# Moving 512 tokens of a two-layer ELU product from plain blocks of 384 to a fourth block in seven products, with a recalibrated planner

## The chip, the cores and the metric

The kernel runs on one core of a Trainium2 chip. The metric is device microseconds for one launch: the median of three runs. A core has TensorE (PE, the matrix products), VectorE (DVE), ScalarE (ACT), GpSimd (POOL) and SyncE (SP, which only issues transfers here). Each engine works through its own list of instructions in order and waits for the others by semaphores.

## The reference

Random-feature attention on 8 x 8 heads of 576 tokens, then a two-layer network with ELU over the 4608 tokens.

```python
def phi(x):                                   # 64 -> 128 features
    proj = np.einsum('bhsd,md->bhsm', x, omega)
    h = proj - np.sum(x * x, axis=-1, keepdims=True) / 2.0
    return np.exp(h - np.max(h, axis=-1, keepdims=True)) / np.sqrt(m)
q_p, k_p = phi(q * scale), phi(k * scale)
kv = np.einsum('bhsm,bhsd->bhmd', k_p, v)
z = np.sum(k_p, axis=2)
attn = np.einsum('bhsm,bhmd->bhsd', q_p, kv) / (np.einsum('bhsm,bhm->bhs', q_p, z)[..., None] + 1e-06)

x = attn as [4608, 512]                       # 8 heads side by side
h = x @ w_in                                  # w_in  [512, 2048]
g = np.where(h > 0.0, h, np.exp(np.minimum(h, 0.0)) - 1.0)
out = g @ w_out                               # w_out [2048, 512]
```

The weights come as 64-bit floats and are converted on the chip. Every product of the network is made from three products of rounded parts: high x high, high x low, low x high.

## The kernel before

**Attention** goes by pairs of heads, 32 pairs (`pair`, i = 0 to 31). For a pair, k and q are projected on PE (`ppk`, `ppq`), a copy of the low part is taken out of PSUM (`p2k`, `p2q`, by ACT or DVE), DVE adds and takes the minimum (line 568), POOL corrects it, ACT makes the exponentials (474). PE makes `pkv`, DVE turns it, two transfers spread it (599, 607). DVE makes the denominators (740), POOL or DVE scales (`norm`), DVE turns the result into `qt` (820) and PE makes `pn` (842), which goes to DRAM as `xd`.

**The network** goes by blocks of tokens. `BLOCKS` names the plain ones: eight of 384 tokens, so that 1536 tokens are left for three blocks of 512 "in seven products". A plain block takes 16 steps (one for each 128 of the 2048 features). In a step, `layer1` makes 12 products `ph` of 384 columns (983 to 985), ACT and DVE make the ELU and its two parts (992 to 1004), and `layer2`, some 3.4 steps later, makes three products of 512 columns into `acc` for each 128 tokens (1017 to 1019), so 9 for a block of 384. The first three blocks go in two halves, SPLIT, while the weights are converted. In the text the plain steps are numbered through: 128 of them before (8 x 16), steps 0 to 47 in the first three blocks.

**A block in seven products** (`units`, `fetch`, `wide1`, `wide2`) makes each product of 2 x 2 sub-blocks with seven products in place of eight. It has 8 steps; a step holds 84 products of 256 columns (1369, 1527, 1339) for 256 features. It needs sums of the weights, made once: `prepare` reads converted `w_in` back into `rw`, makes sums of it and writes `w1t` (16 writes, two for each j = 0 to 7, 1084), through three buffers "raw"; `prepare2` makes sums `tw` of `w_out` in SBUF. `fetch` brings `wp` from `w1s` and `w1t` for each step. `units` makes sums of the tokens (`xw`, `xy`).

**The order** comes from `Plan`. Every piece of work is entered with an engine, a cost in ns, a due time and often a second or third engine with a penalty (`ALT`). `Plan.order` runs through time: at each moment a free engine takes, of what is ready by the planner's own costs, the piece that is due first. What comes out is a fixed list for each engine; the chip then follows these lists. So the costs (`mm`, `act`, `dve`, `pool`, `DMA_LAT`, `DMA_RATE`) and the due times (`PD0` and `PDS` for the pairs, `PREP0` and `PREP`, `TWO0` and `TWO`, `SEG`, `STEP` ...) set nothing but the order and the engine of each piece. In the kernel before, a product of 384 columns was entered at 162.5 ns and one of 512 at 215.8 ns.

Of the kernel before, what the change touches and what calls it, by code (L numbers as in the profile page):

```python
# [62 lines left out]
SUM = 0.873  # L63
UNIT0, UNIT1 = 0.25, 3.77
FETCH = 14.688
BT = [-0.751, -0.373, 0.719, 0.06, 0.525, 0.7, 0.865, -0.155, -0.328, 1.177, -1.344, 0.575, -1.141, 0.489]
AT = (0.0, 0.337, 0.844, 0.312, 0.229, 0.181, 0.386)

LAG = 3.4


PAIR0 = 6.45
DUE_LOAD, DUE_K, DUE_KV, DUE_Q = 9.63, 24.93, 17.79, 16.94
# [1 line left out]
TAIL = 14.17
TAIL2 = -0.54


CONV1 = 13.95
CONV_STEP = 0.16  # L80
CONV2 = 1.14
CONV3 = 41.4
# [1634 lines left out]
```

## Time and profile before

| | us |
|---|---|
| median of 3 runs | 1006.68 (1005.38 to 1009.03) |
| profiled execution | 1008.6 |
| its span, first to last instruction | 1006.8 |
| PE busy in the span | 979.3 |
| DVE busy | 843.7 |
| ACT busy | 766.2 |
| POOL busy | 557.8 |

Matmuls overlap in the profile, so that PE's busy time says that it had work, not that it ran at its pace. The pace is read from the starts of matmuls that follow each other. On DVE and ACT, too, the duration of one instruction is some 0.08 us longer than the distance to the next start when they follow closely. A stretch of the program is looked at by its own row: length, busy time of each engine, clock.

### The profile page before, as it was taken

The page shows a single profiled execution, that of the slowest core. Times are in us where ns is not written, and L with a number is a line of the kernel's source. Part 1 is how long each engine was busy: PE and PEld are TensorE (multiplying, and loading weights), DVE is VectorE, ACT ScalarE, POOL GpSimd, SP SyncE. Part 2 cuts the span into 40 slices and gives each one's busy share as a digit, 9 for nine tenths or more (in the row PEclk, how much of TensorE's full clock was granted, in tenths as well). Part 3 has the DMA queues.
Part 4 walks back from the last instruction along what each step waited for, and adds up shares of the span by engine and source line. Part 5 has one row for each costly group of instructions (what it writes and reads, how often), then busy time and mean ns, then how long its engine had stood idle before and what let it go on. Part 6 is the DMA issues. An engine that isn't in the chain of part 4 may idle for free.

```text
span 1006.8 us, 24315 instructions
## 1 busy us (share of the span) xinstructions
PE 979.3 (97%) x7806; PEld 881.6 (88%) x7806; DVE 843.7 (84%) x3077; ACT 766.2 (76%) x2064; POOL 557.8 (55%) x745
## 2 busy tenths in 40 slices
PE   6999999999999999999999999999999999999997
PEld 5887889888888888888888888887888999999997
DVE  5999978786778967887889888889999889779766
ACT  5999876877568888788887878786555688877774
POOL 0667676776457676677667766685442232223221
PEclk8999999999999999999999999999999999999999
DMA  6656777857766777676776767666888885775762
GB/s 178 181 183 214 238 247 254 270 200 245 232 216 218 232 224 225 202 230 195 252 226 189 242 206 234 203 208 232 268 311 290 289 298 176 238 240 191 239 196 76
DMA packets 93264, 226.27 MB, mean 225 GB/s; under 512 B 23056, under 2 KB 35024, under 8 KB 93136
## 3 DMA queue, kind: packets, MB, share of 16 engines
q1 hardware_dynamic: 93136, 224.70, 69.0%
q8 instruction: 63, 1.03, 0.4%
q14 instruction: 65, 0.53, 0.2%
HBM read 187.43 MB, written 37.22 MB: 223 GB/s over the span
## 4 chain that ended last, share of the span: by engine, by line
PE 69%; DVE 16%; DMA 8%; ACT 3%; issue 2%; SPq 1%; POOL 1%; DVEq 0%; POOLq 0%; ACTq 0%
PE acs L1527 8%; PE ph L983 7%; PE ph L985 6%; PE ph L984 6%; PE acc L1017 6%; PE acc L1018 6%; PE acc L1019 6%; PE A L1369 5%; PE B L1369 4%; PE pn L842 3%; PE pkv L622 2%; PE ppq L554 2%; PE ppk L554 2%; DVE rw L394 2%; DMA rw<-w1s 1%
## 5 line engine op out<-in xcount | busy, mean ns | idle before, releaser
L983 PE MATMUL ph<-xh,w1c 128*128 128x384 f32 x512 | 176.8, 345 | 4.6 <-DVE g L1004 3.0
L984 PE MATMUL ph<-xl,w1c 128*128 128x384 f32 x512 | 172.3, 336 | 1.0 <-DVE xl L807 1.0
L985 PE MATMUL ph<-xh,w1c 128*128 128x384 f32 x512 | 172.3, 336 | 0.0
L1017 PE MATMUL acc<-w2h,g 128*128 128x512 f32 x384 | 154.3, 402 | 0.2
L1018 PE MATMUL acc<-w2l,g 128*128 128x512 f32 x384 | 151.6, 395 | 0.0
L1019 PE MATMUL acc<-w2h,g 128*128 128x512 f32 x384 | 151.5, 394 | 0.0
L983 PEld LDWEIGHTS ph<-xh,w1c 128*128 128x128 f32 x512 | 96.2, 188 | 17.0 <-DVE g L1004 7.3
L984 PEld LDWEIGHTS ph<-xl,w1c 128*128 128x128 f32 x512 | 96.3, 188 | 3.8 <-DVE xl L807 1.4
L992 ACT ACTIVATE e<-ph 128x384 f32<-128x384 f32 x128 | 62.6, 489 | 44.4 <-PE ph L985 43.4
L394 POOL TENSOR_TENSOR hq<-hq,den 128x512 f32<-128x512 f32 (+1 forms) x96 | 81.1, 854 | 27.3 <-DVE den L749 23.5
L985 PEld LDWEIGHTS ph<-xh,w1c 128*128 128x128 f32 x512 | 96.2, 188 | 0.0
L996 DVE SCALAR_TENSOR_TENSOR ph<-e,ph 128x384 f32<-128x384 f32 x128 | 71.2, 556 | 25.5 <-ACT e L993 24.3
L394 POOL TENSOR_TENSOR gq<-yh,gq 128x256 fp32r<-128x256 f32 x49 | 42.7, 871 | 85.1 <-ACT gq L389 67.0
L1019 PEld LDWEIGHTS acc<-w2h,g 128*128 128x128 f32 x384 | 72.1, 188 | 16.9
L1017 PEld LDWEIGHTS acc<-w2h,g 128*128 128x128 f32 x384 | 72.0, 188 | 16.3 <-issue 6.3
L740 DVE CUSTOM_DVE_ANT_0 junk<-hq,pz 128x128 f32<-128x128 f32 (+1 forms) x320 | 74.5, 279 | 11.6 <-PE pz L718 9.3
L394 POOL TENSOR_TENSOR tk<-xk,tk 64x576 fp32r<-64x576 f32 x45 | 64.1, 1424 | 31.5 <-ACT tk L389 12.6
L474 ACT ACTIVATE hk<-hk,nbk 128x128 f32<-128x128 f32 x216 | 68.4, 390 | 17.0 <-POOL nbk L580 16.7
L1018 PEld LDWEIGHTS acc<-w2l,g 128*128 128x128 f32 x384 | 72.1, 188 | 8.6
L474 ACT ACTIVATE hq<-hq,nbq 128x128 f32<-128x128 f32 x216 | 68.5, 391 | 14.4 <-POOL nbq L580 13.6
L394 POOL TENSOR_TENSOR tq<-xq,tq 64x576 fp32r<-64x576 f32 x46 | 65.8, 1431 | 23.6 <-ACT tq L389 11.5
L1004 DVE TENSOR_TENSOR g<-ph,g 128x384 fp32r<-128x384 f32 x128 | 70.4, 550 | 5.7 <-PE pn L842 1.8
(222 smaller groups left out, 2814.7 us busy)
## 6 DMA issues: line engine op xcount, KB each, us to landing
w1c<-w1s SPq DMA_DIRECT2D x112, 512.0 KB, 4.5
wp<-w1t SPq DMA_DIRECT2D x48, 512.0 KB, 4.0
raw_w<-in_w_dram SPq DMA_DIRECT2D x32, 512.0 KB, 4.3
xk<-in_kx_dram SPq DMA_DIRECT2D x24, 576.0 KB, 4.2
xq<-in_qx_dram SPq DMA_DIRECT2D x24, 576.0 KB, 4.7
wp<-w1s SPq DMA_DIRECT2D x24, 512.0 KB, 4.5
v<-in_v_dram SPq DMA_DIRECT2D x32, 325.0 KB, 3.3
w1s<-w1c SPq DMA_DIRECT2D x16, 512.0 KB, 4.2
```

Of the source, the lines that this page charges most:

```text
L394: (nc.vector if e == "DVE" else nc.gpsimd).tensor_tensor(*args)
L474: nc.scalar.activation(h()[:, j, :], src(j), AF.Exp, bias=nb()[:, j:j + 1], scale=-1.0)
L740: nc.vector.tensor_tensor_reduce(out=junk()[r], in0=h()[r, j, :], in1=pz()[r, a * P:(a + 1) * P], scale=1.0, scalar=EPS, op0=ALU.mult, op1 ...
L983: nc.tensor.matmul(ph(), wh, xh[:, c, o:o + n], start=(c == 0), stop=False)
L984: nc.tensor.matmul(ph(), wh, xl[:, c, o:o + n], start=False, stop=False)
L985: nc.tensor.matmul(ph(), wl, xh[:, c, o:o + n], start=False, stop=(c == NC - 1))
L996: lambda: nc.vector.scalar_tensor_tensor(ph(), e()[:, 0:n], -1.0, ph(), ALU.add, ALU.max), (p, e), (p,),
L1017: nc.tensor.matmul(a(), g[0]()[:, ts], w2h[:, f], start=(f == f0), stop=False)
L1018: nc.tensor.matmul(a(), g[0]()[:, ts], w2l[:, f], start=False, stop=False)
L1019: nc.tensor.matmul(a(), g[1]()[:, ts], w2h[:, f], start=False, stop=(f == f1 - 1))
L1369: nc.tensor.matmul(o, at(a, i), u[b][:, i], start=(start and fresh_bank and i == 0 and n == 0), stop=(i == 1 and n == 2), skip_group_check ...
L1527: nc.tensor.matmul(bank()[:, z * TH:(z + 1) * TH], g()[:, a * TH + z * P:a * TH + z * P + P], w(b), start=(j == 0 and z == 0 and m == 0), ...
```

## The change

Plain blocks become six of 384 tokens and one of 256; the tokens left for blocks in seven products become 2048, so four blocks of 512. A plain step of the last block now has 12 products of 256 columns and 6 of 512. There are 112 plain steps. All due times and most penalties are replaced; a product's cost becomes 0.467 n - 6.2 ns (173.1 for 384, 232.9 for 512), POOL's costs rise, a transfer's end is entered later (`DMA_POST`).

```diff
-BLOCKS = [TB] * 8
+BLOCKS = [TB] * 6 + [256]
...
-MLP0 = 37.61
+MLP0 = 26.35
...
-STEP_SA, STEP_S = 9.344, 8.511
-LAG2 = 1.848
-PD0, PDS = 122.22, 19.83
+STEP_SA, STEP_S = 8.851, 9.878
+LAG2 = 17.388
+PD0, PDS = 122.202, 15.999
...
-SLOT = {3: 0, 4: 1, 5: 2, 6: 1, 7: 0}
+SLOT = {3: 0, 4: 1, 5: 2, 6: 0}
...
-PREP0, PREP = -101.339, 8.8
-TWO0, TWO = -37.142, 7.995
+PREP0, PREP = -100.636, 9.727
+TWO0, TWO = -21.196, 7.375
...
+DMA_POST = 2461.004
...
-LOAD2, K2, KV2, Q2 = 61.21, 47.49, 31.23, 34.51
+LOAD2, K2, KV2, Q2 = 55.648, 47.228, 27.084, 26.03
...
-    DMA_LAT, DMA_RATE = 1100.0, 360.0
+    DMA_LAT, DMA_RATE = 500.0, 320.0
...
-                    end[best] = dma + self.DMA_LAT
+                    end[best] = dma + DMA_POST
...
 def mm(n, m=1):
 
-    return m * (n / 2.4 + 2.5)
+    return m * (0.467 * n - 6.2)
...
 def pool(n):
-    return 40 + 2.33 * n
+    return 120 + 2.22 * n
...
-                op("PE", 872 if g < 2 else 240, d, mms, [*((x, a, 2) for a in range(2)), of], (p,))
+                op("PE", 930 if g < 2 else 290, d, mms, [*((x, a, 2) for a in range(2)), of], (p,))
...
-        op("POOL", 3 * pool(2 * M) + 2 * pool(M), due + 0.5, sums, parts, (zs, (zu, 1)))
+        op("POOL", 3480, due + 0.5, sums, parts, (zs, (zu, 1)))
```

The rest of the diff is of this kind: costs of single pieces and the table `ALT`. The lines of the changed kernel stand two lower than before (998 for 996).

In the middle of the plain blocks, DVE's list at the projection of pair 20's q (`hq_20`), before. The copy `p2q_20` out of PSUM isn't in it: ACT has it.

```order
L568 ISA hq_20_6768,nbq_20_6769<-ppq_20_0_6743,p2q_20_0_6762 128x128
L568 ISA nbq_20_6769 128x1
L568 ISA hq_20_6768,nbq_20_6769<-ppq_20_0_6743,p2q_20_0_6762 128x128
L568 ISA nbq_20_6769 128x1
L996 SCALAR_TENSOR_TENSOR ph_71_6714<-e_71_6748,ph_71_6714 128x384
L749 RECIPROCAL den_19_6751<-den_19_6751 128x4
```

The same place after. Plain step 64 stands where step 71 stood, so the pairs come earlier in the plain blocks.

```order
L570 ISA hq_20_6622,nbq_20_6623<-ppq_20_2_6608,p2q_20_2_6627 128x128
L570 ISA nbq_20_6623 128x1
L998 SCALAR_TENSOR_TENSOR ph_64_6524<-e_64_6592,ph_64_6524 128x384
L393 COPY p2q_20_3_6654<-ppq_20_3_6645 128x256
L393 CAST g_64_0_6665<-ph_64_6524 128x384
L570 ISA hq_20_6622,nbq_20_6623<-ppq_20_3_6645,p2q_20_3_6654 128x128
```

A copy `p2q` of this pair has moved from ACT to DVE; of the 96 copies of 256 columns DVE now has 48, against 20 before.

At the end of the plain blocks, DVE's list in steps 122 and 123, before: the ELU of a step (`ph`, two `g`) with the first block's token sums.

```order
L996 SCALAR_TENSOR_TENSOR ph_122_11302<-e_122_11325,ph_122_11302 128x384
L394 TENSOR_TENSOR xw_0_0_11061<-xw_0_1_11148,xw_0_0_11061 128x2x256
L391 CAST g_122_0_11356<-ph_122_11302 128x384
L1004 TENSOR_TENSOR g_122_1_11365<-ph_122_11302,g_122_0_11356 128x384
L394 TENSOR_TENSOR xy_0_11370<-xw_0_1_11148,xw_0_0_11061 128x512
L394 TENSOR_TENSOR xl_148<-xw_0_0_11061,xl_148 128x512
L394 TENSOR_TENSOR xw_0_1_11148<-xw_0_1_11148,xy_0_11370 128x2x256
L394 TENSOR_TENSOR xl_148<-xy_0_11370,xl_148 128x512
L996 SCALAR_TENSOR_TENSOR ph_123_11345<-e_123_11377,ph_123_11345 128x384
```

The same stretch after, in steps 106 to 108 of 256 tokens:

```order
L998 SCALAR_TENSOR_TENSOR ph_106_10728<-e_106_10755,ph_106_10728 128x256
L393 CAST g_106_0_10771<-ph_106_10728 128x256
L396 TENSOR_TENSOR w2_qh_1_156<-tw_4_10725,w2_qh_1_156 128x256
L1006 TENSOR_TENSOR g_106_1_10780<-ph_106_10728,g_106_0_10771 128x256
L396 TENSOR_TENSOR xy_0_10791<-xw_0_1_10574,xw_0_0_10564 128x512
L396 TENSOR_TENSOR w2_qh_1_156<-tw_4_10725,w2_qh_1_156 128x256
L393 CAST xl_148<-xy_0_10791 128x512
L396 TENSOR_TENSOR xw_0_1_10574<-xw_0_1_10574,xy_0_10791 128x2x256
L998 SCALAR_TENSOR_TENSOR ph_107_10775<-e_107_10803,ph_107_10775 128x256
L393 CAST g_107_0_10823<-ph_107_10775 128x256
L1006 TENSOR_TENSOR g_107_1_10833<-ph_107_10775,g_107_0_10823 128x256
L396 TENSOR_TENSOR rw_3_1_10733<-rw_3_1_10733 128x512
```

The pieces of a step are narrower, and weight sums (`tw` for `w2_qh`, `rw`) now stand among the last steps together with the token sums.

In the first block in seven products, SP's list from the last pair of writes of the weight sums (`rw_7`, for step 7) on, before (`wp_0_5_1` is the second transfer for step 5 of block 0):

```order
L1084 DMA w1t_143<-rw_7_0_11792 128x1024
L1084 DMA w1t_143<-rw_7_1_12032 128x1024
L1296 DMA wp_0_5_0_12221<-w1s_142 128x1024
L1296 DMA wp_0_5_1_12260<-w1t_143 128x1024
L1296 DMA wp_0_5_2_12301<-w1t_143 128x1024
L1301 DMA wq_0_7_12348<-w1s_142 128x2x256
L1239 DMA xw_1_0_12358<-xd_144 128x2x512
L1296 DMA wp_0_6_0_12363<-w1s_142 128x1024
L1239 DMA xw_1_1_12373<-xd_144 128x2x512
L1296 DMA wp_0_6_1_12409<-w1t_143 128x1024
```

The same writes after:

```order
L1298 DMA wp_0_6_0_11761<-w1s_142 128x1024
L1298 DMA wp_0_6_1_11794<-w1t_143 128x1024
L1086 DMA w1t_143<-rw_7_0_11469 128x1024
L1086 DMA w1t_143<-rw_7_1_11680 128x1024
L1298 DMA wp_0_6_2_11881<-w1t_143 128x1024
L1303 DMA wq_1_0_11891<-w1s_142 128x2x256
L1241 DMA xw_1_1_11934<-xd_144 128x2x512
L1298 DMA wp_0_7_0_11938<-w1s_142 128x1024
L1298 DMA wp_0_7_1_11963<-w1t_143 128x1024
L1298 DMA wp_0_7_2_12033<-w1t_143 128x1024
```

The writes for step 7 stood ahead of the transfers for step 5; now they stand between those for step 6.

## Rows read from the trace of the kernel before

**Rows 1.** The page, part 1: busy us of each engine.

```profile
PE 979.3 (97%) x7806; PEld 881.6 (88%) x7806; DVE 843.7 (84%) x3077; ACT 766.2 (76%) x2064; POOL 557.8 (55%) x745
```

**Rows 2.** Busy time by stretch: length, PE, PEld, DVE, ACT, POOL, clock, DMA.

```profile
0.00:63.50 63.50, 52.74 (x399) 45.20 (x399) 49.15 (x170) 49.49 (x141) 26.85 (x30) 0.95 0.61 175
63.50:279.60 216.10, 211.03 (x1334) 183.10 (x1333) 181.25 (x588) 166.31 (x406) 144.75 (x156) 1.00 0.72 236
279.60:639.40 359.80, 359.33 (x3166) 315.41 (x3164) 296.23 (x1431) 296.34 (x825) 248.52 (x380) 1.00 0.69 219
639.40:803.90 164.50, 158.94 (x1185) 141.35 (x1185) 151.89 (x472) 103.68 (x278) 81.58 (x113) 1.00 0.78 266
803.90:1006.80 202.90, 197.24 (x1730) 196.53 (x1728) 165.17 (x418) 150.38 (x418) 56.09 (x69) 1.00 0.65 206
842.20:917.90 75.70, 75.39 (x663) 75.18 (x663) 63.95 (x163) 59.12 (x163) 20.71 (x25) 1.00 0.70 224
```

**Rows 3.** The same view, one of the stretches of 20 us.

```profile
720.00:740.00 20.00, 19.65 (x157) 17.41 (x157) 19.41 (x41) 12.29 (x32) 5.89 (x7) 1.00 0.76 283
```

**Rows 4.** Timeline of PE in a plain step: start us, duration us, instruction.

```profile
743.71 0.34 PE L985 MATMUL ph<-xh,w1c 128*128 128x384 f32 x1
743.88 0.39 PE L1017 MATMUL acc<-w2h,g 128*128 128x512 f32 x1
744.11 0.39 PE L1018 MATMUL acc<-w2l,g 128*128 128x512 f32 x1
```

**Rows 5.** Timeline of PE in a block in seven products.

```profile
868.93 0.84 PE L1369 MATMUL A<-xh,wq 128*128 128x256 f32 x6
869.61 0.84 PE L1369 MATMUL B<-xl,wp 128*128 128x256 f32 x6
```

**Rows 6.** The chain that ended last, a pair's larger products: start us, us, what.

```profile
392.99 1.30 PE pn L842 x64
400.41 1.24 PE pkv L622 x20
```

**Rows 7.** Timeline of DVE in the middle of the plain blocks.

```profile
405.37 0.55 DVE L1004 TENSOR_TENSOR g<-ph,g 128x384 fp32r<-128x384 f32 x1
405.84 0.28 DVE L568 CUSTOM_DVE_ANT_0 hk<-ppk,p2k 128x128 f32<-128x128 f32 x1
...
407.85 0.42 DVE L391 COPY p2k<-ppk 128x256 f32<-128x256 f32 x1
408.19 0.70 DVE L820 STREAM_TRANSPOSE qt<-hq 128x512 f32<-128x512 f32 x1
```

**Rows 8.** Groups by line and shape, the copies p2q: count, busy us, mean ns, idle before.

```profile
L389 ACT COPY p2q<-ppq 128x256 f32<-128x256 f32 x76 | 27.7, 367 | 8.7 <-PE ppq L554 8.1
L391 DVE COPY p2q<-ppq 128x256 f32<-128x256 f32 x20 | 8.4, 421 | 5.4 <-PE ppq L554 5.3
```

**Rows 9.** Timeline of DVE, the last transposes of a pair.

```profile
431.24 0.50 DVE L820 STREAM_TRANSPOSE qt<-hq 128x128 f32<-128x128 f32 x2
```

**Rows 10.** Timeline of PE, the product that takes them.

```profile
432.74 1.37 PE L842 MATMUL pn<-qt,zk 32*64 32x160 f32 x64
```

**Rows 11.** Whom PE waited for: us in total, times, longest us.

```profile
PE ph L983 <- DVE g L1004: 3.0, 7, 0.7
...
PE ph L983 <- DMA w1c<-w1s: 0.5, 1, 0.5
```

**Rows 12.** Timeline of SP, three of the writes of weight sums.

```profile
755.83 0.92 SPq L1084 DMA_DIRECT2D w1t<-rw  x2
...
772.43 0.73 SPq L1084 DMA_DIRECT2D w1t<-rw  x1
...
789.67 1.31 SPq L1084 DMA_DIRECT2D w1t<-rw  x1
```

**Rows 13.** Timeline of DVE in the first block in seven products.

```profile
783.73 0.97 DVE L394 TENSOR_TENSOR rw<-rw 128x256 f32<-128x256 f32 x1
...
785.50 0.41 DVE L394 TENSOR_TENSOR rw<-rw 128x256 f32<-128x256 f32 x1
```

More of the change, by code (lines that the diff above doesn't have):

```diff
@@ L47 @@
 NNAT = dict(k=8, q=8)
-MLP0 = 37.61
-SEG = [6.25, 7.76, 3.48, 4.4, 2.75, 6.34]
-STEP = 5.52
-STEP_ATT = 5.44
-STEP_SA, STEP_S = 9.344, 8.511
-LAG2 = 1.848
-PD0, PDS = 122.22, 19.83
+MLP0 = 26.35
+SEG = [6.324, 7.876, 3.468, 4.4, 2.814, 6.61]
+STEP = 5.526
+STEP_ATT = 5.491
+STEP_SA, STEP_S = 8.851, 9.878
+LAG2 = 17.388
+PD0, PDS = 122.202, 15.999
 NSA = 1
-SLOT = {3: 0, 4: 1, 5: 2, 6: 1, 7: 0}
+SLOT = {3: 0, 4: 1, 5: 2, 6: 0}
 NP3 = 29
-PREP0, PREP = -101.339, 8.8
-TWO0, TWO = -37.142, 7.995
[L63 to L73, printed above, removed]
-LOAD2, K2, KV2, Q2 = 61.21, 47.49, 31.23, 34.51
[L75 to L82, printed above, removed]
+PREP0, PREP = -100.636, 9.727
+TWO0, TWO = -21.196, 7.375
+SUM = 1.791
+UNIT0, UNIT1 = 15.907, 4.301
+FETCH = 14.91
+BT = [-0.005, 0.805, 1.476, -0.381, 0.298, -0.265, 1.847, -0.58, -2.137, -0.081, -0.546, -1.317, -1.924, -0.352]
+AT = (0.0, -1.177, 0.709, 0.638, 0.39, 0.064, 0.462)
+LAG = 3.37
+DMA_POST = 2461.004
+PAIR0 = 5.932
+DUE_LOAD, DUE_K, DUE_KV, DUE_Q = 12.998, 24.825, 16.694, 15.838
+LOAD2, K2, KV2, Q2 = 55.648, 47.228, 27.084, 26.03
+TAIL = 11.864
+TAIL2 = -12.969
+CONV1 = 13.966
+CONV_STEP = 0.379
+CONV2 = -1.69
+CONV3 = 44.38
 SPLIT = (0, 8, 16)
 NHALF = 3
-DUE_Z = 15.42
+DUE_Z = 16.328
 NEARLY = 6
@@ L539, in project @@
             op(
-                "POOL", pool(S), due - 4 + a,
+                "POOL", 1495, due - 4 + a,
                 lambda e, r=r, o=o, cs=cs: tt(e, y()[o, cs], x()[r, 0], y()[r, cs].bitcast(F32), ALU.subtract),
@@ L557, in view @@
                 return p().rearrange("p (a x) -> p a x", a=2)
-            op("PE", mm(256, n), d, mms, [(y, a, z) for a in range(2) for z in "hl"] + ["oh", "om"], (p,))
+            op("PE", 118 * n + 10, d, mms, [(y, a, z) for a in range(2) for z in "hl"] + ["oh", "om"], (p,))
             op(
@@ L580, in bias @@
                     nc.gpsimd.tensor_tensor(m, m, q, ALU.subtract)
-                op("POOL", 2 * pool(4), d + 1.3, bias, [sq, *((nb, g, e) for e in range(5))], ((nb, g),))
+                op("POOL", 550, d + 1.3, bias, [sq, *((nb, g, e) for e in range(5))], ((nb, g),))
                 exps(g, js, lambda j: h()[:, j, :], d + 1.5, [(h, g, e) for e in range(5)])
@@ L626, in kv_swapped @@
         parts = parts_of(i, "k")
-        op("PE", 5 * 216, due, mms, [*parts, v], (p,))
+        op("PE", 1340, due, mms, [*parts, v], (p,))
         op("DVE", dve(M), due + 1.2, lambda: nc.vector.transpose(kvf, p()[:, 0:M]), (p,), (("kvf", i % 2),))
@@ L683, in kv @@
         parts = parts_of(i, "k")
-        op("PE", 220, due, last, [*parts, v], ((p, 0), (p, 1)))
+        op("PE", 240, due, last, [*parts, v], ((p, 0), (p, 1)))
         for a in range(2):
@@ L776, in finish @@
             d = due - 5 + g
-            op("PE", 109 * n, d, turn, ((h, "n", g),), (p,))
+            op("PE", 115 * n + 20, d, turn, ((h, "n", g),), (p,))
             op(
@@ L796, in finish @@
         d = due - 2
-        op("PE", 4 * mm(S) + 200, d, mms, [*((qh, g) for g in range(3)), ("kvf", i % 2)], [p for _, _, p in halves])
+        op("PE", 1250, d, mms, [*((qh, g) for g in range(3)), ("kvf", i % 2)], [p for _, _, p in halves])
         for half, (qs, n, p) in enumerate(halves):
@@ L846, in output @@
         op(
-            "PE", 4 * mm(4 * N) + 200, due, mms, [*((qt, g) for g in range(3)), *((zk, "kv", e) for e in range(4))], banks
+            "PE", 1400, due, mms, [*((qt, g) for g in range(3)), *((zk, "kv", e) for e in range(4))], banks
         )
```

4 lines of the change are left out of this document (2 added, 2 removed).

## The prediction

> **What bounds the kernel now.** The page's busy times come first: PE 97%, DVE 84%, ACT 76% [rows 1]. A busy PE need not run at its pace, so I then read the starts of matmuls. In a plain step a product of 384 columns is followed after 0.17 us and one of 512 after 0.23 us [rows 4]; the medians of all such distances are 0.174 and 0.233. In the blocks in seven products six products of 256 columns take 0.68 us, 0.113 each [rows 5]. A pair's `pn` and `pkv` take 1.30 and 1.24 us [rows 6], its 18 projections and `pz` about 0.12 each: 4.9 us.
>
> Then the span by stretches [rows 2], cut where PE begins plain steps 0, 40 and 104 and step 4 of the first block in seven products. I call them A to E (the last row of the group is one whole block in seven products and belongs to E). Counting PE's instructions at their pace gives the work in each, and the rest is lost:
>
> A 44.4 of 63.5, lost 19.1. B 203.3 of 216.1, lost 12.8. C 353.2 of 359.8, lost 6.6. D 154.4 of 164.5, lost 10.1. E 195.9 of 202.9, lost 7.0. Together 951.2 of work and 55.6 lost.
>
> So PE is the bound from the first plain step on. Where DVE has room, PE loses under 2%: in C DVE is busy 296 of 360, 82%. In D it is busy 151.9 of 164.5, 92%, and PE loses 6.5% [rows 2]. That pair of rows carries the prediction.
>
> **The work that goes and comes on PE.** A plain step of 384 tokens is 12 x 0.174 + 9 x 0.233 = 4.185 us; two blocks are 32 steps, 133.9 us, which go. The block of 256 brings 16 steps of 12 x 0.113 + 6 x 0.233 = 2.754 us, 44.1. The fourth block in seven products brings 75.7, read off a whole one [rows 2]. Net 44.1 + 75.7 - 133.9 = -14.1 us. The matmuls are f32 at one pace in both kernels, the clock stands at 1.00 (2.4 GHz) from the first plain step on [rows 2], and no stretch of the change would lower it. This gain is sure as work; the question is how much more PE waits.
>
> **DVE in the middle.** The order puts the pairs closer: before, one pair for 3.65 plain steps; after, one for 2.9 (20 pairs in steps 40 to 95, where it was 18 in steps 40 to 103). PE work of the new C (steps 40 to 95), counted over the list: 56 x 4.185 + 20 x 4.9, some 333 us. DVE: a step's three passes of 384 at 0.47 us [rows 7] are 1.41, 56 of them 79 us. What is left of the old C's 296 after 64 x 1.41 = 90 is 206, over 18 pairs 11.4 each; 20 pairs are 229. To these come the pieces that the new list hands to DVE: 28 copies `p2q` of 0.34 us [rows 7, 8], and ten subtractions of 576 columns that POOL had, about 1.0 each, so 20 us over 24 pairs, 16 here. Sum 79 + 229 + 16 = 324 us, 97% of PE's 333 (it was 82%). ACT, counted likewise, comes to 90%.
>
> What PE would lose at that load: below, the old C's 1.9% (6.6 us); above, the old D's 6.5% (21.7 us). Reasons for the lower end: the chain from a pair's last `ppq` to its `pn` was long before because due times made it so, and `pn` came 1 to 2 us after the last transpose was done (431.24 + 0.50 to 432.74) [rows 9, 10]; counted over the new list, 20.5 us of PE work lie between the two (28.8 before) with 16.1 us of DVE work (21.4 before), 79% against 74%: tighter, but not by much. I take 9 us lost, 2 to 3 above the old C.
>
> **DVE at the change of stage.** The new D runs from plain step 96 to the end of the first block in seven products. PE work there: 16 x 2.754 + 75.7 + the rest of the last pairs and of the block before, counted 125.4. DVE, counted over the list: 16 for the steps, 7 for the last pairs, 51 for the weight sums `rw` and `tw`, 16 for token sums, 45 for the seven products; 135, and 139.9 by the ratio that the old D has (147 counted, 151.9 busy). Here DVE has more to do than PE, because the weight sums are as many as before while the plain steps that hid them are 8 fewer and narrower. DVE can be busy 97% while PE is busy 98% [rows 3], so 139.9 takes 144 at the least; PE may be ahead by about a plain step, 3 us. I take 141.5, lost 16, where the old D lost 10.1. Ends: 136 (lost 11, some of the sums run over into the second block, whose stretch has room: DVE 64 of 75.7 [rows 2]) and 151.5 (lost 26, DVE at the old D's 92%).
>
> **The rest.** A and B hold the same attention work: DVE 57 and 171 us counted against 58 and 167, PE 44.4 and 201.7 against 44.4 and 203.3; at most 2 us either way, priced +0.5. One more block in E adds what the middle ones lose, under 0.5. The later ends of transfers in the planner move only SP's order; PE waited for weights 0.5 us in all [rows 11], so this part is worth nothing by itself. POOL stays under 85%.
>
> By the span: 1006.8 - 14.1 + 2.5 + 6 + 0.5 + 0.5 = 1002.2. The profiled execution lay 1.8 above its span and 1.9 above the median of the runs, so 1002 in those terms, and I round the ends' drift into **1001.5 us**.
>
> **Weight sums on SP.** After, the writes for step 7 stand between the transfers for step 6; before, ahead of those for step 5. The sums came every 17 us (755.83, 772.43, 789.67) [rows 12], while a step takes 9.5. SP waits in order, so a late `rw` holds `wp` behind it, and PE with it. The new order leaves about 1.5 steps less between a write and its reader, some 14 us. I price it at nothing, hidden by the half step that is left and by the transfers already fetched; if this cover is gone it costs up to 9 us: the last three sums at 17 us are 51, and the new list gives them 4.5 steps, 42.
>
> **Rivals.** *The lists tell true* (18%): the new list's PE costs, 173 and 233 ns, are those of the trace, so pieces are placed where they are really ready, C loses no more than before, and DVE's excess in D runs over into the second block. 1006.8 - 14.1 + 1 + 1 = about 994.5. Against it: 97% on DVE.
>
> *It cancels* (20%): C loses 14 and D 18, 1006.8 - 14.1 + 7.5 + 8 = 1008: no change that can be measured.
>
> *DVE takes over, slower* (17%): DVE keeps only the 92.3% of the old D. C takes 324 / 0.923 = 351, lost 18, D 151.5, lost 26: 1006.8 - 14.1 + 11.5 + 16 = 1020. It decides from the point where DVE's busy share of C stays under 95% although PE has gaps. For it: all three engines are above 90% there, with two `ph` banks between them.
>
> *The SP queue* (6%): 9 us in the first block in seven products on top of the forecast, 1010.
>
> *DVE blocked by POOL* (7%): of two DVE pieces `rw` of one shape one took 0.97 us, the other 0.41 [rows 13]. If 20 more of the weight sums meet such a neighbour in the new D, where DVE is the bound, at 0.55 each that is 11 us, 1012. The Trainium skill, page "SBUF — State Buffer", section "SBUF: two separate sides", names what could do it: a DVE instruction with two inputs in SBUF and a GpSimd instruction that reads SBUF contend for one pair of ports, and the later one waits for the whole of the other. The trace agrees as far as the pair of durations above goes.
>
> *It does not do what it says*: excluded for the blocks (the list holds 112 plain and 32 steps of seven products); true for the late transfers, which is priced at nothing.
>
> **How the numbers follow.** My forecast, 996 to 1003.7, has 32%, the better rival 18%, together 50% for faster by over 0.3%; within 0.3% (about what a measurement of this kernel can tell from no change) 20%; slower 30% from the last three rivals. Range 989 to 1020: below lies the case where A and B gain too, above the one where DVE and SP both fail. The likeliest case's own range is 994 to 1008.
>
> **What would show it.** Right: plain steps 40 to 95 take 339 to 346 us with DVE at 93% or more; from step 96 to the second block in seven products 136 to 146; a middle block 75.7; the stretch to plain step 40 within 3 us of 279.6. Wrong: PE waiting for DVE pieces (`g`, `qt`) by more than 20 us in C, or for `wp` in the first block in seven products; or DVE's pieces much longer than before at the same shapes.

## The result and the profile after

The changed kernel takes 1020.62 us (median of 4 runs, 1020.26 to 1023.59), the kernel before 1006.24 beside it: a ratio of 1.0144, 95% interval 1.0117 to 1.0172. It is slower by 1.4%, clear of the noise, where 1001.5 was forecast, and lies 0.6 us above the range. The profiled execution took 1023.59 with a span of 1021.8, 15.0 more than before.

Page of the changed kernel, part 1 (busy us of each engine, to be laid beside [rows 1]):

```profile
PE 980.9 (96%) x8094; PEld 882.1 (86%) x8094; DVE 907.6 (89%) x3255; ACT 787.6 (77%) x2144; POOL 561.3 (55%) x747
```

PE is busy as long as before, but does less: counted at its pace its list holds 937.8 us, 13.4 fewer than 951.2. DVE is busy for 64 us more.

Busy time by stretch in the changed kernel, A to E as the prediction cuts them and then D in four parts (columns as in [rows 2]):

```profile
0.00:63.20 63.20, 52.72 (x399) 45.23 (x399) 48.77 (x170) 51.20 (x143) 25.60 (x29) 0.95 0.63 183
63.20:278.60 215.40, 209.41 (x1331) 181.72 (x1330) 187.34 (x600) 173.28 (x421) 145.51 (x160) 1.00 0.71 235
278.60:627.10 348.50, 345.50 (x3235) 297.48 (x3235) 324.60 (x1586) 297.28 (x851) 266.65 (x416) 1.00 0.69 224
627.10:780.60 153.50, 138.13 (x1085) 123.69 (x1083) 144.20 (x381) 97.09 (x268) 59.60 (x70) 0.99 0.81 281
780.60:1021.80 241.20, 235.11 (x2052) 233.96 (x2052) 202.72 (x523) 168.78 (x462) 63.93 (x73) 0.99 0.63 203
627.10:665.30 38.20, 33.18 (x299) 26.38 (x298) 36.75 (x132) 23.08 (x68) 20.05 (x28) 1.00 0.83 297
665.30:688.80 23.50, 20.97 (x125) 18.38 (x124) 21.77 (x45) 9.39 (x24) 10.36 (x12) 0.93 0.72 248
688.80:737.00 48.20, 42.02 (x323) 38.91 (x322) 44.91 (x108) 31.32 (x85) 14.86 (x17) 1.00 0.90 307
737.00:780.60 43.60, 41.96 (x345) 40.02 (x343) 40.77 (x100) 33.30 (x93) 14.33 (x13) 1.00 0.75 255
```

Work counted over PE's list, and what is lost against it:

| | work | took | lost | lost before |
|---|---|---|---|---|
| A | 44.4 | 63.2 | 18.8 | 19.1 |
| B | 201.7 | 215.4 | 13.7 | 12.8 |
| C | 333.9 | 348.5 | 14.6 | 6.6 |
| D | 125.4 | 153.5 | 28.1 | 10.1 |
| E | 232.4 | 241.2 | 8.8 | 7.0 |

So -13.4 of work, +18.0 in D, +8.0 in C, and 2.4 in the rest: +15.0.

Whom PE waited for in D of the changed kernel (us in total, times, longest us):

```profile
PE ph L985 <- DVE g L1006: 6.4, 4, 2.5
PE A L1371 <- ACT c L391: 2.0, 2, 1.6
PE A L1371 <- DVE g L1006: 1.2, 1, 1.2
```

The waits that the trace counts are some 14.5 us, 12 of them on DVE and 2.5 on ACT, none on a transfer. After the longest of them the granted clock of steps 104 to 111 was 0.93 instead of 1.00 (the second part of D above): between the two levels that is 14% of 23.5 us, 3.3 us, at 1.2 GHz, or 1.6 us of work.

In C the same view counts 2.6 us of waits, none of them for DVE's `g` or `qt`; two of its lines:

```profile
PE ph L985 <- ACT qt L391: 1.6, 3, 0.9
PE ppk L556 <- POOL tq L396: 0.4, 1, 0.4
```

So the 14.6 us lost in C are hardly waits that the view names. By the starts of PE's matmuls about two thirds of them lie in pauses of under 0.15 us each beyond the usual distance of two products, which that view leaves out; what ends these pauses is not shown.

### The profile page after: what moved, and what is told of

Its sections match the earlier page's. It is cut to its first block, busy times and chain, and to the rows that moved or that the text cites. A ratio compares the mean times of both kernels' runs of the same rounds, so it can differ in the third digit from the quotient of the medians.

```text
span 1021.8 us, 25269 instructions
## 1 busy us (share of the span) xinstructions
PE 980.9 (96%) x8094; PEld 882.1 (86%) x8094; DVE 907.6 (89%) x3255; ACT 787.6 (77%) x2144; POOL 561.3 (55%) x747
## 4 chain that ended last, share of the span: by engine, by line
PE 68%; DVE 16%; ACT 8%; DMA 3%; issue 2%; POOL 1%; SPq 1%; DVEq 0%; ACTq 0%; POOLq 0%
PE acs L1529 11%; PE A L1371 7%; PE acc L1019 6%; PE ph L985 6%; PE acc L1020 5%; PE B L1371 5%; PE acc L1021 5%; PE ph L987 5%; PE ph L986 5%; PE ppk L556 2%; PE pkv L624 2%; PE pn L844 2%; PE ppq L556 2%; DVE rw L396 2%; ACT hq L476 2%
## 5 line engine op out<-in xcount | busy, mean ns | idle before, releaser
L985 PE MATMUL ph<-xh,w1c 128*128 128x384 f32 (+1 forms) x448 | 150.8, 337 | 10.0 <-DVE g L1006 8.1
L987 PE MATMUL ph<-xh,w1c 128*128 128x384 f32 (+1 forms) x448 | 147.4, 329 | 0.0
L986 PE MATMUL ph<-xl,w1c 128*128 128x384 f32 (+1 forms) x448 | 147.3, 329 | 0.0
L1019 PE MATMUL acc<-w2h,g 128*128 128x512 f32 x320 | 130.1, 407 | 0.6 <-DVE g L393 0.6
L1021 PE MATMUL acc<-w2h,g 128*128 128x512 f32 x320 | 127.0, 397 | 0.8 <-DVE g L1006 0.8
L1020 PE MATMUL acc<-w2l,g 128*128 128x512 f32 x320 | 126.7, 396 | 0.0
L985 PEld LDWEIGHTS ph<-xh,w1c 128*128 128x128 f32 x448 | 84.3, 188 | 21.5 <-DVE g L1006 12.4
L994 ACT ACTIVATE e<-ph 128x384 f32<-128x384 f32 (+1 forms) x112 | 53.0, 474 | 46.7 <-PE ph L987 39.7
L987 PEld LDWEIGHTS ph<-xh,w1c 128*128 128x128 f32 x448 | 84.4, 188 | 0.0
L1529 PE MATMUL acs<-w2h,gq 128*128 128x256 f32 x384 | 80.0, 278 | 1.6 <-DVE gq L396 1.0
L998 DVE SCALAR_TENSOR_TENSOR ph<-e,ph 128x384 f32<-128x384 f32 (+1 forms) x112 | 59.9, 536 | 19.6 <-ACT e L995 19.2
L932 POOL TENSOR_TENSOR u_w<-u_w,raw_w 128x512 int32<-128x512 int32 x32 | 43.8, 1368 | 60.5 <-DVE u_w L929 55.6
L1529 PEld LDWEIGHTS acs<-w2h,gq 128*128 128x128 f32 x384 | 64.2, 188 | 2.5 <-DVE gq L396 1.7
```

Source lines behind the costliest of these rows:

```text
L985: nc.tensor.matmul(ph(), wh, xh[:, c, o:o + n], start=(c == 0), stop=False)
L986: nc.tensor.matmul(ph(), wh, xl[:, c, o:o + n], start=False, stop=False)
L987: nc.tensor.matmul(ph(), wl, xh[:, c, o:o + n], start=False, stop=(c == NC - 1))
L998: lambda: nc.vector.scalar_tensor_tensor(ph(), e()[:, 0:n], -1.0, ph(), ALU.add, ALU.max), (p, e), (p,),
L1019: nc.tensor.matmul(a(), g[0]()[:, ts], w2h[:, f], start=(f == f0), stop=False)
L1020: nc.tensor.matmul(a(), g[0]()[:, ts], w2l[:, f], start=False, stop=False)
```

## The experiments

Lost time is again what a stretch took less PE's work counted over that kernel's own list. Where a stretch has a granted clock under 1.00, part of what it lost is the clock, worked out as above. C is always plain steps 40 to 95, "the change of stage" step 96 to the end of the first block in seven products (the changed kernel's D). On this cut the kernel before loses 5.8 in C (318.0 us) and 10.9 at the change of stage. Ratios are to the kernel before, run beside; the changed kernel's is 1.0144. Those two rows of the kernel before:

```profile
279.60:597.60 318.00, 317.53 (x2801) 278.45 (x2799) 262.85 (x1264) 260.43 (x722) 219.69 (x336) 1.00 0.70 220
597.60:842.20 244.60, 239.04 (x1888) 216.53 (x1886) 218.91 (x725) 171.58 (x470) 121.94 (x171) 1.00 0.75 253
```

The runs of 1 to 3 keep every engine's list as it is but for the pieces named. Those of 4 and 5 change what the planner is given, so all lists are drawn up anew, and such a run compares whole orders.

**1. Is DVE the bound? Work added to it.** One reduction of 512 columns that nothing waits for (0.68 us, some 0.60 to the next start), 16 times; I call it a dose.

```diff
+    def dose():
+        nc.vector.tensor_reduce(spare, ident.unsqueeze(1).to_broadcast([P, 4, P]), AX.X, ALU.min)
...
             def ttr(c=c, n=n, p2=p2, view=view):
+                if nm == "k" and c == 0 and 13 <= i < 29:
+                    dose()
```

In the middle of the kernel before:

> The kernel before, with 16 more DVE instructions (a minimum over 128x512 into a spare 128x4 tile, some 0.6 us each by the reduction of the same shape, 9.6 us together), one at the projection of k of each of the pairs 13 to 28, in the middle of the plain blocks. Theory 'DVE is the bound where its share passes about 93%': DVE goes from 82% to 85% of that stretch, PE still sets the pace, so 0 to +2 us (1006 to 1008). Rival 'any added DVE work shows, because the two engines walk in lockstep': +5 to +10 us (1011 to 1016).

In the middle of the changed kernel:

> The changed kernel with the same 16 DVE instructions at the same pairs (9.6 us). There DVE is busy 324.6 of 348.5 us, 93%. Theory 'DVE is the bound there': +5 to +9 us (1025 to 1030). Rival 'PE's own order loses the time there and DVE has room': 0 to +3 us (1020 to 1024).

In the changed kernel beside the ACT copies of `prepare`:

> The changed kernel with the same instruction 16 times, one ahead of each of the two conversions of each weight sum rw (9.6 us), most of them between plain step 96 and the second block in seven products, where DVE is busy 144 of 153.5 us. Theory 'DVE is the bound there': +8 to +10 us (1028 to 1031). Rival 'the way of the sums through memory and SP's list is the bound': +1 to +4 us, since each sum takes 1.2 us longer but two are under way at once. Rival 'narrow steps on PE': 0.

Measured: 1.0074 (1.0045 to 1.0103), 1.0232 (1.0209 to 1.0256) and 1.0252 (1.0226 to 1.0279); the medians are 1014.16, 1030.06 and 1031.11 us. The first lies where the rival had it, the other two 0.1 us above what was expected. The stretches that took the doses, in the kernel before steps 40 to 103 (359.8 us without the doses), then C and D of the changed kernel (348.5 and 153.5):

```profile
281.30:643.80 362.50, 361.53 (x3166) 315.18 (x3164) 303.69 (x1447) 295.63 (x825) 248.13 (x380) 1.00 0.68 217
```

```profile
277.00:633.00 356.00, 348.59 (x3236) 297.22 (x3235) 333.78 (x1602) 297.81 (x851) 267.40 (x416) 1.00 0.67 219
```

```profile
625.30:786.10 160.80, 140.03 (x1083) 124.92 (x1081) 152.72 (x399) 97.55 (x268) 61.40 (x70) 0.98 0.77 269
```

In the middle of before, 9.6 us more on DVE made the stretch 2.7 us longer (28%); the rest of the 7 us by which the whole grew is scattered over stretches that hold no dose, and in the stretch itself the rival is not borne out. In the changed kernel's C it was 7.5 of 9.6 (78%), in its D, which holds 14 of the doses, 7.3 of some 8.4 (87%). There DVE's list stands on the path; before it mostly did not.

**2. Work taken off DVE.** First, the arithmetic of `prepare`, 29 us of DVE, left out, with 10 us of ACT's conversions and 4 us of POOL's additions and subtractions for the same sums (one of the lines is shown); then the copies `p2q` given to ACT where they stand.

```diff
...
-                tt(x, o, p, q, alu)
+                return
...
```

> The changed kernel without the arithmetic of prepare (the sums and their split into two parts, 29 us on DVE, 10 on ACT, 4 on POOL are left out; the transfers and the order of all else stay). Theory 'DVE is the bound from plain step 96 to the second block in seven products': DVE there falls from 144 to some 117, below PE's 125; the stretch goes from 153.5 to 130 to 135, the total to 999 to 1003. Rival 'way through memory and SP': the transfers stay, so the stretch gains under 8 us, 1013 to 1018. Rival 'narrow steps on PE': no change, 1019 to 1022.

```diff
...
-                "ACT", act(n * M, True), d + 0.5, lambda e, n=n, p2=p2, view=view: copy(e, p2()[:, 0:n], view()[:, 0:n, M:]),
+                "ACT", act(n * M, True), d + 0.5, lambda e, n=n, p2=p2, view=view: copy("ACT" if nm == "q" else e, p2()[:, 0:n], view()[:, 0:n, M:]),
...
```

> The changed kernel with all p2q copies on ACT, at their places in the order: DVE has about 19 us less, ACT 17 more, most of it in the middle. DVE theory: the middle loses half of its 14.6 us, 1012 to 1017. Rival (any engine in order at 90% does it, ACT as well as DVE): 1019 to 1026.

D without the sums, and C with the copies on ACT:

```profile
624.80:766.70 141.90, 132.64 (x1084) 121.09 (x1082) 116.15 (x325) 90.05 (x254) 55.91 (x71) 1.00 0.88 304
```

```profile
276.80:632.80 356.00, 348.38 (x3235) 298.98 (x3235) 313.04 (x1534) 308.32 (x899) 268.31 (x416) 1.00 0.65 219
```

Without the sums 1.0043 (1.0023 to 1.0062), 1010.91 us, 8 above the expected: D gives 11.6 us, but still loses 16.5 with DVE at 82%. With the copies on ACT 1.0251 (1.0227 to 1.0275), 1029.78 us, beyond even the rival: with 11.6 us less on DVE and 11.0 more on ACT, C takes 7.5 us longer. "DVE's load is the bound" is thus half of the story in D, and not the whole rule in C: there added DVE work shows (the doses), but work moved to ACT shows too, with ACT's busy share at 87% instead of 85 and DVE's at 88% instead of 93. No run takes work off DVE in C without giving it to ACT.

**3. GpSimd's reads.** Its additions and subtractions for the second weights' sums and the first block in seven products become fills; then each fill three times over, as long as the arithmetic it replaces (the edit below); the same in the kernel before; and with the sums of `prepare` left out as well.

```diff
+    def quiet(e, dst, *args):
+        if e == "POOL":
+            for _ in range(3):
+                nc.gpsimd.memset(dst.bitcast(F32) if dst.dtype == F32R else dst, 0.0)
+        else:
+            tt(e, dst, *args)
...
-                "POOL", pool(TH), due + at, lambda eng: tt(eng, x(o), x(p), x(q), alu), ((t, p), (t, q)), ((t, o),),
+                "POOL", pool(TH), due + at, lambda eng: quiet(eng, x(o), x(p), x(q), alu), ((t, p), (t, q)), ((t, o),),
...
```

> The changed kernel with GpSimd's additions and subtractions for the second weights' sums and for the first block in seven products replaced by fills with zero, so that GpSimd reads no SBUF there; this arithmetic is left out. Contention theory: of the 15.9 us by which DVE pieces are longer than their shape's base at the change of stage half goes, and that stretch gives 4 to 7 us: 1013.5 to 1017. If DVE is long for another reason: within 1019.5 and 1021.5.

> As the run with GpSimd's reads off (the same arithmetic left out), but each fill three times over, 3 x 0.315 = 0.95 us, so that GpSimd is busy there as long as with its subtractions (0.72 to 1.09 us). If it is the reading that holds DVE up: DVE's busy time at the change of stage stays near 132 us, the stretch at 143 to 147, the whole at 1011 to 1015. If the gain of 7.6 us came of GpSimd's results being there sooner: the stretch back at 150 or more, 1017 to 1021.

> The kernel before with the same fills in the same places (the same arithmetic left out). Its DVE pieces at the change of stage are 10.2 us longer than their shapes' base (15.9 in the changed kernel), and DVE has more PE work beside it. If contention is part of what the change costs: it gains 3 to 5 us here (ratio 0.995 to 0.997), less than the changed kernel's 7.6. If it gains 7 or more, contention costs both kernels alike and explains none of the difference.

> The changed kernel with the fills and without the arithmetic of the first weights' sums (both left out), so DVE at the change of stage has some 105 to 110 us for PE's 125. If the loss there is DVE's work and contention: that stretch takes 131 or less, the whole 998 to 1002. If narrow plain steps or the first steps in seven products lose by their own chain from engine to engine: 136 to 141, 1005 to 1010.

Measured: 1.0081 (1.0057 to 1.0104), 1.007 (1.0048 to 1.0091), 0.9975 (0.9954 to 0.9997) and 1.0007 (0.9987 to 1.0026); in us 1012.98, 1013.89, 1004.43 and 1008.88. With one fill D took 144.0 us: it gave 9.5, where 4 to 7 were expected. D with three fills, where POOL is busy for 62.02 us instead of 59.60:

```profile
627.60:772.40 144.80, 133.16 (x1084) 121.38 (x1083) 132.09 (x382) 97.32 (x269) 62.02 (x189) 1.00 0.87 298
```

D is 8.7 us shorter, and DVE does the same pieces in 132.09 instead of 144.20. Groups of DVE's sums in D, of the changed kernel and then with the fills (count, busy us, mean ns):

```profile
L396 DVE TENSOR_TENSOR rw<-rw 128x512 f32<-128x512 f32 x14 | 11.9, 855 | 0.1
L396 DVE TENSOR_TENSOR rw<-rw 128x256 f32<-128x256 f32 x21 | 10.6, 503 | 0.0
```

```profile
L403 DVE TENSOR_TENSOR rw<-rw 128x512 f32<-128x512 f32 x14 | 9.5, 681 | 1.0 <-DMA rw<-w1s 1.0
L403 DVE TENSOR_TENSOR rw<-rw 128x256 f32<-128x256 f32 x21 | 8.8, 418 | 0.0
```

One of these, on the timelines of DVE and of POOL in the changed kernel (start us, us):

```profile
635.35 1.22 DVE L396 TENSOR_TENSOR rw<-rw 128x512 f32<-128x512 f32 x1
```

```profile
634.13 1.89 POOL L396 TENSOR_TENSOR w_ld<-tw,w_ld 128x256 fp32r<-128x256 f32 x2
635.98 1.19 POOL L396 TENSOR_TENSOR tw<-w2h,w2l 128x256 f32<-128x256 f32 x1
```

The DVE piece lasts 1.22 us in place of 0.68: it began 0.67 us before POOL's ended. POOL's fills of the same length hold nobody up, so it is the reading, as the contention rival had it. The Trainium skill, page "SBUF — State Buffer", section "SBUF: two separate sides", says that a DVE instruction with two inputs in SBUF and a GpSimd instruction that reads SBUF wait for each other's end; it is borne out with 144.20 - 132.09 = 12.1 us of DVE time here. The kernel before gains 2.5 us in all, less than the 3 to 5 expected, and 2.1 in its D, which took 162.4 us instead of 164.5 with DVE at 146.56 instead of 151.89:

```profile
636.30:798.70 162.40, 158.41 (x1186) 141.14 (x1185) 146.56 (x474) 103.82 (x278) 85.87 (x197) 1.00 0.78 270
```

So some 6 of the 8.7 belong to the change.

Without reads and sums D, in the same four parts and whole:

```profile
626.60:662.70 36.10, 32.28 (x297) 26.14 (x296) 28.82 (x116) 21.57 (x65) 21.96 (x63) 1.00 0.90 309
662.70:682.10 19.40, 19.36 (x124) 17.29 (x125) 15.16 (x35) 7.91 (x21) 10.94 (x37) 1.00 0.95 332
682.10:725.90 43.80, 40.45 (x323) 38.13 (x321) 31.59 (x88) 29.45 (x83) 17.58 (x58) 1.00 0.95 327
725.90:765.80 39.90, 39.84 (x343) 39.29 (x343) 32.19 (x86) 31.24 (x90) 10.43 (x33) 1.00 0.82 284
626.60:765.80 139.20, 131.92 (x1084) 120.85 (x1082) 107.76 (x324) 90.17 (x255) 60.90 (x190) 1.00 0.90 311
```

13.8 us are still lost with DVE at 77%, as the rival with the narrow steps had it. But by parts (work 29.8, 18.6, 38.2, 38.8) they are 6.3, 0.8, 5.6 and 1.1: the eight narrow steps that stand alone lose next to nothing, the eight that stand beside the last pairs do. In the changed kernel the same parts lose 8.4, 4.9, 10.0 and 4.8. The kernel before was not run without the sums, so how much of the 5.6 us between these two runs belongs to the change is open.

**4. The narrow steps.** The block of 256 placed fourth, and the changed kernel with a third PSUM bank for it.

```diff
-BLOCKS = [TB] * 6 + [256]
+BLOCKS = [TB] * 3 + [256] + [TB] * 3
```

> The changed kernel with its block of 256 tokens fourth instead of last (steps 48 to 63), so the last 16 plain steps are of 384 and stand beside the weight sums. The work is the same on each engine. Theory one, narrow steps lose by themselves because what follows a product on ACT and DVE has less PE work to hide behind: steps 48 to 63 take over 10% longer than PE's count and the whole stays at 1017 to 1024. Theory two, the loss at the change of stage comes of DVE work that is too much for so little PE work: there the loss falls from 28 to 10 us or less; the middle, whose PE work falls by 23 us and DVE work by 7, becomes DVE-bound and gives back 8 to 15, in all 1010 to 1018.

```diff
-        p = Buf(ps, [P, 512], F32, "ph", f"ph_{F}", 2)
+        p = Buf(ps, [P, 512], F32, "acc2", f"ph_{F}", 1) if blk == NBLK - 1 and f % 3 == 2 else Buf(ps, [P, 512], F32, "ph", f"ph_{F}", 2)
```

> The changed kernel, in whose block of 256 every third step's product goes to the third accumulator's bank, which that block leaves unused, so three banks instead of two stand between PE and the elementwise work. Bank theory: the 16 narrow steps lose 13.3 us now and 7 or less then, the whole 1012 to 1016. If DVE's load alone sets them (94% busy there): 12 or more lost there, or as much more in the first block in seven products, 1018 to 1022.

Measured 1.0273 (1.0244 to 1.0303) and 1.02 (1.0161 to 1.024), 1031.83 and 1027.64 us: both are longer than any theory had it. With the block early, steps 48 to 63:

```profile
337.70:423.60 85.90, 77.74 (x792) 65.38 (x791) 78.48 (x417) 74.28 (x225) 67.18 (x108) 0.96 0.73 247
```

PE's work there is 68.8, so 17.1 us are lost, 1.1 for each narrow step, where the same steps at 384 lose 5.4 in the changed kernel; some 3 of the 17.1 are the granted clock of 0.96. C in all loses 34, the change of stage 18.6 instead of 28.1:

```profile
622.50:786.50 164.00, 154.38 (x1117) 141.19 (x1116) 149.55 (x376) 98.34 (x264) 57.04 (x73) 0.99 0.76 265
```

Narrow steps beside pairs lost in both places where they were tried. The parts of D with the third bank:

```profile
625.70:663.20 37.50, 34.20 (x305) 27.17 (x303) 35.86 (x128) 22.30 (x66) 21.35 (x30) 1.00 0.86 300
663.20:685.50 22.30, 19.10 (x118) 15.73 (x119) 21.12 (x47) 8.76 (x23) 8.32 (x10) 1.00 0.80 276
685.50:740.10 54.60, 44.34 (x310) 40.32 (x309) 45.04 (x111) 32.08 (x85) 17.79 (x18) 0.94 0.79 272
```

With it the narrow steps lose 11.4 instead of 13.3, and the first half of the block in seven products 17.9 instead of 10.0, some 3 of it by the clock of 0.94. A third bank did not bring the 7 or less that the bank theory asked for. But the planner drew other lists for it on every engine, so the run does not show what a third bank would do to the lists of the changed kernel.

**5. The blocks without the planner, the planner without the blocks, and the pace of the pairs.** The new planner with the old blocks (the edit below), and the old planner with the new blocks and pairs every 16.0 us (the old `PDS` of 19.83 cannot be ordered with them; no pace between the two was run with the new blocks):

```diff
-BLOCKS = [TB] * 6 + [256]
+BLOCKS = [TB] * 8
-SLOT = {3: 0, 4: 1, 5: 2, 6: 0}
+SLOT = {3: 0, 4: 1, 5: 2, 6: 1, 7: 0}
```

> The changed kernel with the old blocks (eight of 384 tokens, three blocks in seven products) and all else of the change: planner costs, late transfers, due times, pairs every 16 us. PE's work is the old 951 us. Theory, the loss belongs to the block of 256 (16 narrow steps beside as many weight sums): the change of stage has its eight wide blocks of cover back and loses about 10 us as in the kernel before, the middle, with the dense pairs, some 12 instead of 6.6: 1007 to 1014. Rival, the loss belongs to the new order itself: the 28 us that PE waits more in the changed kernel come here too, 1022 to 1036. If the planner is right by itself: under 1004.

> The kernel before with the new blocks and pairs every 16.0 us, all else of the old planner (costs, due times, no late transfers). If the middle's loss comes of the pace of the pairs: steps 40 to 95 lose 13 to 16 us as in the changed kernel, the whole 1016 to 1023. If it comes of the new planner's order: they lose 6 to 9, the whole 1008 to 1015. The change of stage loses 25 to 30 either way.

Old blocks with other paces (`PDS` alone), and with the new due times but the old costs:

> Eight blocks of 384 with the new planner, and pairs every 17.9 us, between the 16.0 of the changed kernel and the 19.83 of before. If the pace of the pairs sets what the middle loses: steps 40 to 95 lose some 9 us (14 at 16.0, 6.6 in the middle of before), and the change of stage, with a pair or two more, 4 to 6 instead of 2: 1002 to 1007, at best below the kernel before. If the middle loses 14 again the pairs' pace is not what costs: 1008 to 1012.

> The kernel before with pairs every 16.0 us instead of 19.83 and nothing else. Pace theory: steps 40 to 95 lose 13 to 16 us (some 5 in the kernel before), from step 96 on 5 less is lost: 1008 to 1013. Order theory: steps 40 to 95 lose 6 to 9 and the rest 5 less: 1001 to 1005.

> The kernel before with pairs every 17.9 us. Pace theory: steps 40 to 95 lose 9 to 12, 1005 to 1010. Order theory: 6 to 8, and the change of stage 3 to 5 less than before: 1001 to 1005, at best a gain that can be measured.

> Eight blocks of 384, the new due times and pairs every 16.0 us, but the planner's costs and transfer ends of before. If the costs (PE's 173 and 233 ns, late transfers) are what makes the dense pairs bearable: steps 40 to 95 lose 30 or more, 1025 to 1050. If the due times are: 12 to 18 lost there, 1005 to 1013.

> Eight blocks of 384 with the new planner and its due times, pairs every 19.83 us as in the kernel before. If the new order has a price of its own at any pace: steps 40 to 95 lose 12 or more, where the kernel before loses 6, and the whole is 1010 or more. If the pace alone sets the middle's loss: 6 to 8 there, 1003 to 1008.

The new planner with old blocks (e5), C and the change of stage; the old planner at 16.0 with old blocks (e15), the same two, and with the new blocks (e14), the same two:

```profile
275.80:623.90 348.10, 345.45 (x3237) 297.63 (x3236) 321.99 (x1593) 296.51 (x849) 265.96 (x414) 1.00 0.67 221
623.90:841.20 217.30, 214.30 (x1450) 197.73 (x1449) 180.14 (x425) 120.03 (x298) 65.75 (x77) 1.00 0.72 252
```

```profile
281.30:664.80 383.50, 360.02 (x3220) 307.59 (x3219) 315.77 (x1541) 302.68 (x881) 277.77 (x427) 0.97 0.64 201
664.80:881.10 216.30, 212.05 (x1444) 195.22 (x1443) 174.22 (x408) 118.98 (x302) 56.35 (x69) 1.00 0.75 253
```

```profile
277.80:663.40 385.60, 361.56 (x3222) 308.88 (x3221) 314.36 (x1516) 302.51 (x877) 284.09 (x433) 0.97 0.66 206
663.40:816.60 153.20, 134.24 (x1071) 123.48 (x1070) 138.80 (x388) 94.27 (x265) 52.07 (x60) 0.94 0.78 272
```

C of e16, e12, e18 and e17:

```profile
276.10:611.30 335.20, 329.89 (x2956) 289.07 (x2955) 283.99 (x1397) 280.45 (x805) 244.66 (x377) 1.00 0.69 220
```

```profile
275.60:611.80 336.20, 329.59 (x2993) 285.45 (x2991) 306.89 (x1441) 273.94 (x772) 228.45 (x363) 1.00 0.69 218
```

```profile
277.00:605.40 328.40, 323.53 (x2836) 281.30 (x2836) 279.46 (x1308) 257.38 (x726) 219.33 (x338) 1.00 0.66 213
```

```profile
281.20:653.80 372.60, 356.34 (x3247) 303.99 (x3246) 311.44 (x1569) 301.91 (x868) 276.73 (x426) 0.99 0.66 207
```

| planner, pairs every | blocks | ratio (interval) | C lost | DVE in C | change of stage lost |
|---|---|---|---|---|---|
| old, 19.83 (before) | old | 1 | 5.8 | 83% | 10.9 |
| old, 17.9 (e16) | old | 1.0038 (1.0014 to 1.0063) | 11.8 | 85% | 10.6 |
| old, 16.0 (e15) | old | 1.0405 (1.0371 to 1.0439) | 49.7 | 82% | 7.2 |
| old, 16.0 (e14) | new | 1.057 (1.0527 to 1.0613) | 51.2 | 82% | 32.9 |
| new, 16.0 (e5) | old | 1.0054 (1.0033 to 1.0075) | 13.7 | 93% | 5.1 |
| new, 16.0 (changed kernel) | new | 1.0144 (1.0117 to 1.0172) | 14.6 | 93% | 28.1 |
| new, 17.9 (e12) | old | 1.0093 (1.0061 to 1.0125) | 16.7 | 91% | 7.0 |
| new, 19.83 (e18) | old | 1.0322 (1.0285 to 1.0359) | 12.8 | 85% | 31.9 |
| new due times, old costs, 16.0 (e17) | old | 1.0295 (1.0253 to 1.0337) | 36.1 | 84% | 5.9 |

What PE waited for in C with the old planner at 16.0 (e15):

```profile
PE pn L842 <- DVE den L740: 8.6, 5, 2.7
PE ph L983 <- DVE g L1004: 3.1, 4, 1.3
```

The table's outcomes against what was expected: e5, e17 and e18 went as one of their theories had it, e16 as the pace theory (0.3 us above its total), and e12, e14 and e15 as neither, 5, 42 and 35 us above the higher one. Four things follow.

- The new blocks lose 23 us more at the change of stage under the new planner (28.1 against 5.1) and 26 under the old (32.9 against 7.2, of which some 9 are e14's clock of 0.94 there), against 13.4 of PE work saved. So by themselves they cost more than they save: 9 of the change's 14 us (1.0054 to 1.0144), and 17 under the old planner (1.0405 to 1.057). The other 5 are there with the old blocks (e5).
- Pairs at 16.0, the pace that comes with the change, cost the old planner 50 us in C. The waits that the view counts there are some 21 us, of which a pair's denominators are the largest group with 8.6; the granted clock of 0.97 is another 11 or so.
- The new planner brings the 50 down to 14: its due times and penalties with the old costs still lose 36, its costs, with the later transfer ends, do the rest.
- With the old blocks it loses 13 to 17 in C at every pace tried (e5, e12, e18). So this goes with its order and not with the pairs' pace, as one theory of e12 had it; what in the order does it is not shown.

In e18 the total is off by something that neither theory saw: 23 us in one place, steps 112 to 119, where `pn` waited 9.7 us for DVE's `qt` and `pz` 5.5 for POOL's `zk`, and where the granted clock was 0.83, which is 21 of the 61.7 us at 1.2 GHz (the row stands at the end). The late pairs meet the weight sums, whose due times stayed (`rw` and `tw` are 24.6 us of DVE's work between 700 and 745 there; that they caused the wait is inferred, not tried). The median of e12 lies 4 us above its profiled execution, so its stretches may be a few us short.

No kernel here that does the whole computation beats the kernel before.

## Why the prediction was wrong

- **PE's work**, -14.1: measured -13.4. Right.
- **A, B and E**, +1.0: measured +2.4. Right in kind; E lost 1.8 more than before, for 0.5 forecast.
- **SP's queue**, priced at nothing: no wait of PE in D ended at a transfer. Right, and the rival of 6% did not come.
- **C's counts** were right: DVE 324 counted, 324.60 busy; PE 333 and 333.9 (the 97% set against 82% there mixes two bases: of PE's work, as the 97% is, it was 84%). **C's loss** was mis-sized: 9 forecast, 14.6 measured. The step that failed is the scale: it read what PE loses off DVE's busy share, between the old C's 1.9% and the old D's 6.5%. The measured 4.4% of its work lies between them, but that doesn't bear the scale out: at 82% DVE, e15 loses 15% of its work (some 3 points of it by the clock), and with 11.6 us moved from DVE to ACT (e7) C grew. DVE's busy share alone does not set the loss; the same work in another order of the lists loses 50 us or 14 (e15, e5).
- **D**, the larger miss: +6 forecast, +18.0 measured. The failing sentence is that DVE "can be busy 97%" over the whole stretch because it was over 20 us [rows 3]; it was 94%. The pieces themselves were mis-sized too: 139.9 forecast, 144.20 measured, and 132.09 without GpSimd's reads. And some 2.7 us were taken off for PE running a step ahead of DVE, which the measured stretch does not give back. In the prediction's own sum the 12 us between 141.5 and 153.5 are 4.4 for the pieces, 4.8 for the share and 2.7 for the step. The ratio 151.9/147 with which 135 became 139.9 (139.5 by the digits shown) already was contention: without GpSimd's reads the old D has DVE busy for 146.56 (e10). It grew to 144.20/135; why is not shown. Of D's 28.1, 8.7 go with the reads (e9), 5.6 more with the sums (e11). Of the 13.8 left, 11.9 lie beside the last pairs and in the first four steps in seven products, and the prediction had no term for them: it counted the narrow steps' work, 2.754 each, and gave them no loss of their own. How much of the 13.8 the kernel before has too, in the 10.9 of its change of stage, is not shown.
- **The clock**: "no stretch of the change would lower it" was wrong for steps 104 to 111, at 0.93, but that is 1.6 us of work.
- **The signs**: the stretch to step 40 came as said (278.6), C lies 2.5 us above its span of 339 to 346, D 7.5 above 136 to 146. Of the signs of being wrong, PE's waits for DVE's pieces in C did not come (2.6 us of waits in all), and DVE's longer pieces at the same shapes did (`rw` of 512 columns 855 ns in D, 743 in the kernel before).
- **The rivals.** "DVE takes over, slower" gave C 351, D 151.5 and 1020, and 348.5, 153.5 and 1020.6 came: the number was right, and so was the side, at 17%. Its own sign came, DVE under 95% of C, at 93%. Its mechanism, DVE as the bound at 92%, holds in D in part (e3, e4); in C the doses speak for it (e2), and e7 and e15 against DVE's load as the whole of it. So the total is in part luck. "DVE blocked by POOL", held at 7% for 11 us, is real: 8.7 us in D, some 6 of them more than in the kernel before. They were added up as exclusive cases, but both came at once.
- **The planner's costs** were weighed as one rival ("the lists tell true") and otherwise as nothing. With the new due times in place they are worth 24 us (e17 against e5, 1.0295 to 1.0054). The prediction took the dense pairs' price off the finished list, and so never saw that two large effects stood against each other: new blocks with dense pairs cost 57 us under the old planner, the new planner gives 43 of them back.

What stays open: why a narrow step beside pairs loses 0.8 to 1.1 us, and why the new planner's C loses 13 to 17. Reads and sums are excluded as the whole cause of the first (e11), and a third bank didn't cure it, in other lists (e13); the likeliest, an inference, is that the pairs' pieces stand in ACT's and DVE's lists between a step's product and its `g`, and a step of 2.75 us hides less of them than one of 4.19. No run separates that.

## What to carry to other kernels

Shrinking the bound engine's work pays only as far as the other engines' in-order work beside it still has cover: count work for each engine in the stretch that gets shorter, and where a second engine comes out above the first (144 against 125 here), price the stretch, as a first estimate, at the second engine's busy share of a like stretch, not at its best 20 us. Count with durations under contention when GpSimd reads there at the same time. And a busy share is no scale for what the first engine loses elsewhere: doses on each engine, or a list with one cost changed, tell what stands on the path.
